# Agent attention with a SoLU layer: every second pair of token tiles takes another way from the activations to the output

## The chip, the cores and the metric

The kernel runs on one NeuronCore of a Trainium2 chip. Five engines work side by side and wait for each other through semaphores: TensorE (PE in the profile, its weight loads PEld) multiplies matrices into PSUM; VectorE (DVE) and ScalarE (ACT) read PSUM and SBUF; GpSimd (POOL) works on SBUF only; SyncE (SP) issues the transfers, which 16 DMA engines carry out. Each engine works through its instructions in the order in which they were written. The metric is the device time of one execution in microseconds (us), as the median of several runs; lower is better.

## The reference

Four batches of 12608 tokens of 128 numbers go through an attention with 49 agents per batch, and the 50432 resulting rows through a feed-forward layer with 1024 hidden columns. All is fp32.

```python
def _attn_ref(q, k, v, agents):
    def sm(a, b):
        s = scale * (a @ b.transpose(0, 2, 1))
        s = s - s.max(-1, keepdims=True)
        e = np.exp(s)
        return e / (e.sum(-1, keepdims=True) + 1e-09)
    agent_v = sm(agents, k) @ v
    return sm(q, agents) @ agent_v

def _moe_ref(x, w_in, w_out, g_ln):
    h = x @ w_in
    e = np.exp(h - np.max(h, axis=-1, keepdims=True))
    solu = h * e / (np.sum(e, axis=-1, keepdims=True) + 1e-09)
    mu, var = mean and variance of solu over its 1024 columns
    return ((solu - mu) / np.sqrt(var + 1e-06) * g_ln) @ w_out
```

## The kernel before

**Phase A**, once per batch: the agents against k and v, in 13 chunks of up to 1024 tokens. Its result is multiplied into `w_in`, so that the first layer becomes one product of 49 attention weights with a matrix of 1024 columns (`bmats`, kept as a high and a low part, `mh` and `ml`). **Phase B**, per 8 tiles of 128 tokens: the attention weights p of each token, turned by TensorE (`pack` to a PSUM bank `px`), split by ScalarE (`b6`, L698) and VectorE (`b7`, L703) into a high and a low part `pn`, and laid into `pT` by four transfers (`b8`, L716).

**Phase C**, per tile of 128 tokens (396 of them), is where the time goes: `c_h` multiplies `pT` with `mh` and `ml` into a PSUM pair `ph` (L757); `c_max` takes the row maximum on VectorE (L761); `c_exp` the exponentials on ScalarE (L771); `c_u` the product u of both on VectorE (L776); `c_sq` the squares on ScalarE (L782). There are two `ph`, so at most two tiles are between their first product and their u. Then u must be turned, so that the 1024 hidden columns lie along the partitions: `c_t` does it with 8 TensorE transposes per tile (L789), into `px` banks, of which there are four. From there u goes to SBUF in a high part `uH` and a low part `uL`. For most halves ScalarE copies (`c_ev`, L808), and GpSimd splits (`c_sph` L817, `c_spl` L821); for the halves named in `DIR` ScalarE writes `uH` itself (L804) and VectorE subtracts (`c_ldir`, L813). `c_w` then multiplies a pair of tiles (256 tokens) with the output weights: 24 products, high by high, low by high and high by low for each of the 8 slices of 128 columns (L837), with the weights stationary. The output comes out with its 128 columns along the partitions. Four tiles are a group: `c_rstd` makes the scale of each token on GpSimd, `sent` brings it through DRAM to all partitions (`dr`, `rB`, L878 and L879), `c_fin` multiplies it in while it empties the bank (L902), `c_out` stores (L918).

**The order of everything** is written out in advance. A planner (`Plan`) takes every operation with its engine, its cost, what it depends on and a due time, counted in tiles, and lays the operations one after the other on each engine; the order of PE, ACT, DVE and POOL is then fixed as it was laid. The due times are constants in the kernel (`BD0` to `DWL`), one for each kind of operation. SP issues its transfers in order too, each held back until what it waits for has happened.

## Time and profile before

The median of three runs is 1538.96 us (1538.89 to 1542.58).

| What | Value |
|---|---|
| span of the profiled execution, first to last instruction | 1535.9 us |
| median of the runs less that span | 3.1 us |
| busy: PE, ACT, DVE, POOL | 1509.6, 1424.4, 1366.4, 1251.6 us |
| mean granted TensorE clock | 0.998 |
| DMA queue q1, share of 16 engines | 33.0% |
| bytes moved | 159.65 MB |

The profiled execution's own time is known by its span alone; 3.1 us is what lies around it if it was a run like the median. A busy PE is a modelled figure: products are pipelined, and the end of each is computed. How fast they follow each other is read from their starts, in the timeline. In the groups the columns are line, engine, operation, output and inputs with their sizes, count, then busy time in us and the mean of one in ns, and idle time of that engine ahead of them.

### The profile page before, as it was taken

The page shows a single profiled execution, that of the slowest core. Times are in us where ns is not written, and L with a number is a line of the kernel's source. Part 1 is how long each engine was busy: PE and PEld are TensorE (multiplying, and loading weights), DVE is VectorE, ACT ScalarE, POOL GpSimd, SP SyncE. Part 2 cuts the span into 40 slices and gives each one's busy share as a digit, 9 for nine tenths or more (in the row PEclk, how much of TensorE's full clock was granted, in tenths as well). Part 3 has the DMA queues.
Part 4 walks back from the last instruction along what each step waited for, and adds up shares of the span by engine and source line. Part 5 has one row for each costly group of instructions (what it writes and reads, how often), then busy time and mean ns, then how long its engine had stood idle before and what let it go on. Part 6 is the DMA issues. An engine that isn't in the chain of part 4 may idle for free.

```text
span 1535.9 us, 35549 instructions
## 1 busy us (share of the span) xinstructions
PE 1509.6 (98%) x12643; PEld 1352.4 (88%) x12643; DVE 1366.4 (89%) x2201; ACT 1424.4 (93%) x2747; POOL 1251.6 (81%) x1613
## 2 busy tenths in 40 slices
...
GB/s 371 190 128 73 146 91 111 96 101 94 95 77 151 111 111 90 139 82 104 82 97 136 106 118 87 128 99 104 68 89 61 87 66 90 72 86 56 63 56 46
DMA packets 114720, 159.65 MB, mean 104 GB/s; under 512 B 16240, under 2 KB 71152, under 8 KB 114544
## 3 DMA queue, kind: packets, MB, share of 16 engines
q1 hardware_dynamic: 114544, 157.39, 33.0%
q8 instruction: 100, 1.64, 0.4%
q14 instruction: 76, 0.62, 0.1%
...
## 4 chain that ended last, share of the span: by engine, by line
PE 73%; ACT 9%; POOL 7%; DVE 5%; issue 4%; DMA 2%; DVEq 0%; SPq 0%; ACTq 0%; POOLq 0%
PE px L837 28%; PE ph L757 18%; PE px L789 17%; ACT e L771 4%; POOL uL L821 3%; PE px L476 2%; PE px L427 2%; PE px L657 2%; ACT sq L782 2%; POOL uH L817 2%; ACT uT L808 2%; DVE u L776 1%; PE px L460 1%; PE px L692 1%; POOL y L856 1%
## 5 line engine op out<-in xcount | busy, mean ns | idle before, releaser
L821 POOL TENSOR_TENSOR uL<-uT,uH 128x1024 fp32r<-128x1024 f32 (+1 forms) x344 | 661.9, 1924 | 25.3
L761 DVE TENSOR_REDUCE nm<-ph 128x1 f32<-128x1024 f32 x396 | 479.2, 1215 | 73.9 <-PE ph L757 72.5
L776 DVE SCALAR_TENSOR_TENSOR u<-ph,e 128x1024 f32<-128x1024 f32 x396 | 480.4, 1218 | 41.9 <-ACT e L771 31.1
L782 ACT ACTIVATE sq<-u,su 128x1024 bf16<-128x1024 f32 x396 | 463.7, 1171 | 23.0 <-DVE u L776 19.7
L771 ACT ACTIVATE e<-ph,nm 128x1024 f32<-128x1024 f32 x396 | 449.0, 1137 | 16.9 <-DVE nm L761 15.3
L837 PE MATMUL px<-uL,wH 128*128 128x256 f32 x1584 | 461.6, 291 | 1.3 <-POOL uL L821 1.3
L837 PE MATMUL px<-uH,wH 128*128 128x256 f32 x1584 | 451.9, 285 | 4.2 <-DVE uL L813 2.0
L837 PE MATMUL px<-uH,wL 128*128 128x256 f32 x1584 | 448.8, 283 | 0.0
L789 PE MATMUL px<-ident,u 128*128 128x128 f32 x3168 | 430.1, 273 | 2.8 <-DVE u L776 1.6
L789 PEld LDWEIGHTS px<-ident,u 128*128 128x128 f32 x3168 | 365.2, 141 | 40.1 <-DVE ob L902 2.5
L757 PE MATMUL ph<-mh,pT 128*128 128x512 f32 x792 | 334.3, 422 | 5.2 <-DMA pT<-pn 2.4
L817 POOL TENSOR_SCALAR uH<-uT 128x1024 fp32r<-128x1024 f32 (+1 forms) x344 | 298.5, 868 | 46.8 <-ACT uT L808 44.7
L837 PEld LDWEIGHTS px<-uH,wH 128*128 128x128 f32 x1584 | 298.8, 189 | 19.4 <-issue 5.7
L808 ACT COPY uT<-px 128x512 f32<-128x512 f32 x541 | 301.6, 592 | 13.0 <-PE px L789 4.8
L757 PE MATMUL ph<-ml,pT 128*128 128x512 f32 x792 | 313.0, 395 | 0.1
L837 PEld LDWEIGHTS px<-uL,wH 128*128 128x128 f32 x1584 | 298.9, 189 | 7.9 <-issue 3.0
L837 PEld LDWEIGHTS px<-uH,wL 128*128 128x128 f32 x1584 | 299.0, 189 | 5.5 <-issue 1.4
L813 DVE TENSOR_TENSOR uL<-px,uH 128x512 fp32r<-128x512 f32 x251 | 167.9, 683 | 9.9 <-ACT uH L804 9.2
L757 PEld LDWEIGHTS ph<-mh,pT 128*128 128x128 f32 x792 | 149.6, 189 | 30.6 <-issue 6.8
L757 PEld LDWEIGHTS ph<-ml,pT 128*128 128x128 f32 x792 | 150.2, 190 | 16.5 <-DVE ml L552 0.6
L804 ACT CAST uH<-px 128x512 fp32r<-128x512 f32 x251 | 147.2, 606 | 2.4 <-PE px L789 2.0
L856 POOL TENSOR_TENSOR y<-x,nhalf 128x4 f32<-128x4 f32 x99 | 100.1, 1011 | 7.7
...
## 6 DMA issues: line engine op xcount, KB each, us to landing
...
```

The source lines that it names most:

```text
L757: nc.tensor.matmul(ph[:, sl], lhs, bmats[b]["mh" if m == 0 else "ml"][:, sl], start=(m == 0), stop=(m == 1))
L761: nc.vector.tensor_reduce(out=nms[x], in_=phs[x], op=ALU.max, axis=AX.X, negate=True)
L771: nc.scalar.activation(out=es[x], in_=phs[x], func=AF.Exp, bias=nms.pop(x), accum_out=st[G]["S"][:, j : j + 1])
L776: nc.vector.scalar_tensor_tensor(out=u, in0=phs[x], scalar=INV, in1=es[x], op0=ALU.mult, op1=ALU.mult, accum_out=su)
L782: nc.scalar.activation(out=sq, in_=u, func=AF.Square, bias=su, scale=-float(DF), accum_out=st[G]["Q"][:, j : j + 1])
L789: nc.tensor.transpose(pt[:, kf * P : (kf + 1) * P], us[x][0][:, k0 * P : (k0 + 1) * P], ident)
L804: nc.scalar.copy(out=uH, in_=pt)
L808: nc.scalar.copy(out=rr[x][:, hf * 4 : hf * 4 + 4, :], in_=pt)
L813: nc.vector.tensor_tensor(out=uL, in0=pt, in1=uH.bitcast(F32), op=ALU.subtract)
L817: nc.gpsimd.tensor_scalar(out=uH, in0=rr[x][:, k0:k1, :], scalar1=1.0, scalar2=0.0, op0=ALU.mult, op1=ALU.add)
L821: nc.gpsimd.tensor_tensor(out=uL, in0=rr[x][:, k0:k1, :], in1=uH.bitcast(F32), op=ALU.subtract)
L837: nc.tensor.matmul(po, wt[:, kf, :], ut[:, kf, :], start=(q == 0), stop=(q == WM - 1))
```

## The change

Pairs of tiles are now of two kinds, taken in turn (`PAT`): Z pairs keep the way described above, Y pairs take a new one. By the instructions of the changed kernel 204 tiles are Z and 192 are Y. Two pairs of one kind make a group of four tiles, so a group spans three pairs of the order, and groups of the two kinds overlap.

For a Y tile, `c_tb` has VectorE turn u in blocks of 32 by 32 in one instruction of 128x1024 elements (SBUF to SBUF, L866). When four Y tiles are turned, `c_mv` issues 16 transfers from SBUF to SBUF, each of 32 partitions by 4 KB, 2.1 MB together, which bring the blocks to the right partitions (`uY`, L873). `c_wy` then multiplies in native fp32: a slice of turned u of 128 hidden columns by 128 tokens is stationary, the fp32 weights `w2` move; 32 products per group in chunks of two (L879). The output has tokens along the partitions; its scale per token is fetched by `c_yp` (one store, four loads of single numbers, L885 and L887), multiplied in by `c_fy` on ScalarE (L894, 31 groups, four instructions each) or VectorE (L896, 17 groups), and stored to a second output by `c_oy` (four stores per group, L905). The rows of the two outputs are put together after the run.

Z tiles lose the direct halves except within the last ten tiles: GpSimd splits all of them. In phase B, `b6` copies to fp32 (L743) and GpSimd makes both parts of p (`b7h` L749, `b7l` L754). Buffers change: k and v have one chunk instead of two, `uH`/`uL` two instead of four, `uT` three instead of four, `pT` four instead of eight. Every due time has a new value; the diff shows one of them.

```diff
+PAT = "ZYZY"
...
+def pair_kinds(n):
+
+    kinds = ["Z" if i < HEADZ or i >= n - 4 else PAT[i % len(PAT)] for i in range(n)]
+    if kinds.count("Y") % 2:
+        kinds[max(i for i in range(n) if kinds[i] == "Y")] = "Z"
+    units, open_ = [], {}
+    for i, k in enumerate(kinds):
+        if k in open_:
+            units[open_.pop(k)][1].append(i)
+        else:
+            open_[k] = len(units)
+            units.append((k, [i]))
+    return units
...
-    UTB = 4
...
+    UTB = 3
+    ZB = 2
+    SB = 6
+    DIR = {(1, 0), (1, 1), (3, 1), (5, 0), (5, 1), (7, 1)}
+    DT0 = 10.8
...
-    DH = -3.24
...
+    DH = -9.08
...
-    PTB = 8
...
+    PTB = 4
...
+    B7G = True
...
-    kpool = ctx.enter_context(tc.tile_pool(name="kpool", bufs=2))
+    kpool = ctx.enter_context(tc.tile_pool(name="kpool", bufs=1))
...
-    gpool = ctx.enter_context(tc.tile_pool(name="gpool", bufs=4))
+    gpool = ctx.enter_context(tc.tile_pool(name="gpool", bufs=ZB))
+    ypool = ctx.enter_context(tc.tile_pool(name="ypool", bufs=2))
...
+    w2 = const.tile([P, NF, C], F32, name="w2")
...
-                old = M1.get(c - 2) if not head else M1.get(c - 7 - c % 2)
+                old = M1.get(c - 1) if not head else M1.get(c - 5 - c % 4)
...
-            nc.scalar.copy(out=r["n", q][:, 0, :w], in_=r["pt", q][:, :w])
+            if B7G:
+                r["f", q] = bpool.tile([P, GT // 2 * P], F32, tag="pf", bufs=2, name=f"pf{b}_{t0}_{q}")
+                nc.scalar.copy(out=r["f", q][:, :w], in_=r.pop(("pt", q))[:, :w])
+            else:
+                nc.scalar.copy(out=r["n", q][:, 0, :w], in_=r["pt", q][:, :w])
+
+        def b7h(q):
+            w = (min(GT, nt - q * GT) + 1) // 2 * P
+            nc.gpsimd.tensor_scalar(out=r["n", q][:, 0, :w], in0=r["f", q][:, :w], scalar1=1.0, scalar2=0.0, op0=ALU.mult, op1=ALU.add)
+
+        def b7l(q):
+            w = (min(GT, nt - q * GT) + 1) // 2 * P
+            pn = r["n", q]
+            nc.gpsimd.tensor_tensor(out=pn[:, 1, :w], in0=r.pop(("f", q))[:, :w], in1=pn[:, 0, :w].bitcast(F32), op=ALU.subtract)
...
+            if B7G:
+                d7 = op("G", lambda q=q: b7h(q), 0.38, dues[5] + 2.5 * q + B7, [a6])
+                d7 = op("G", lambda q=q: b7l(q), 0.7, dues[5] + 2.5 * q + B7 + 0.01, [d7])
...
+    def c_tb(x):
+        G, j = slot[x]
+        if G not in yb:
+            yb[G] = [ypool.tile([P, GT, NF, GT, SQB], F32, tag="tb", name=f"tb{G}"), None]
+        to = yb[G][0][:, :, :, j, :].rearrange("p r k c -> p k r c")
+        nc.vector.transpose(to, us[x][0].rearrange("p (k r c) -> p k r c", r=GT, c=SQB))
+
+    def c_mv(G):
+        tb = yb[G][0]
+        to = yb[G][1] = ypool.tile([P, GT, NF, GT, SQB], F32, tag="uY", name=f"uY{G}")
+        for a in range(GT):
+            for r in range(GT):
+                nc.sync.dma_start(out=to[SQB * r : SQB * (r + 1), a], in_=tb[SQB * a : SQB * (a + 1), r])
+
+    def c_wy(G, a, k0, px=None):
+        if px is not None:
+            st[G]["po"] = px
+        for kf in range(k0, k0 + YC):
+            nc.tensor.matmul(st[G]["po"][:, a * P : (a + 1) * P], yb[G][1][:, a, kf].rearrange("p x c -> p (x c)"),
+                             w2[:, kf, :], start=(kf == 0), stop=(kf == NF - 1))
+
+    def c_yp(G):
+        dr = dpool.tile([P, GT], F32, tag="dy", name=f"dy{G}")
+        yp = st[G]["yp"] = tiny.tile([P, GT], F32, tag="yp", name=f"yp{G}")
+        nc.sync.dma_start(out=dr, in_=st[G]["y"])
+        for x in range(GT):
+            nc.sync.dma_start(out=yp[SQB * x : SQB * (x + 1), :], in_=dr.rearrange("(a c) x -> x c a", c=SQB)[x])
+
+    def c_fy(G, e):
+        ob = obs[G] = opool.tile([P, GT, P], F32, tag="oy", name=f"oy{G}")
+        po, y = st[G]["po"], st[G]["yp"]
+        if e == "A":
+            for j in range(GT):
+                nc.scalar.mul(out=ob[:, j, :], in_=po[:, j * P : (j + 1) * P], mul=y[:, j : j + 1])
+        else:
+            nc.vector.tensor_tensor(out=ob, in0=po.rearrange("p (j d) -> p j d", d=P),
+                                    in1=y.unsqueeze(2).to_broadcast([P, GT, P]), op=ALU.mult)
+
+    def c_oy(G):
+        for z, i in enumerate(units[G][1]):
+            for q in range(2):
+                b, t = divmod(2 * i + q, TB)
+                x, lo = 2 * z + q, (0 if t < TB - 1 else TB * P - N)
+                c0 = b * N + min(t * P, N - P)
+                nc.sync.dma_start(out=out_t[c0 + lo : c0 + P, :].rearrange("(a c) d -> c a d", c=SQB),
+                                  in_=obs[G][SQB * x : SQB * (x + 1), lo // SQB :, :])
+
     def direct(x, hf):
-        return (x % (2 * GT), hf) in DIR or x >= n - TD
+        return (x % (2 * GT), hf) in DIR and x >= n - DT0 or x >= n - TD
...
+        if isY:
+            TBT[x] = op("D", F(c_tb, x), 1.15, at(x, DTB, DTBR, DTBL), [U[x], MV.get(back(G, 2))])
+            if j == GT - 1:
+                a = [TBT[2 * z + q] for z in units[G][1] for q in range(2)]
+                MV[G] = op("S", F(c_mv, G), (5.5, 2.1, 0), x + DMV, a + [WY.get(back(G, 2))])
+                prev = None
+                for q in range(GT * NF // YC):
+                    a, k0 = divmod(q * YC, NF)
+                    f = (lambda px, G=G: c_wy(G, 0, 0, px)) if q == 0 else F(c_wy, G, a, k0)
+                    prev = op("P", f, 0.219 * YC, x + DWY + DWS * q / (GT * NF // YC), [MV[G], prev, FY.get(back(G, 2)) if q == 0 else None] + wready, take=q == 0)
+                    if q == 0:
+                        lead_y = prev
+                WY[G] = prev
...
+            buf = [W.get((zpairs[zix[i] - ZB], 1)) if zix[i] >= ZB else None]
...
+            if isY:
+                YP[G] = op("S", F(c_yp, G), (1.9, 0, 5.0), x + DR, [o, FY.get(back(G, 2))])
+                FY[G] = op("AD", F(c_fy, G), (1.45, 0.62), x + DFY, [WY[G], YP[G], OY.get(back(G, 2))], free=lead_y)
+                OY[G] = op("S", F(c_oy, G), (1.5, 0, 2.5), x + DFY, [FY[G]])
...
-    nc = _bacc.Bacc("TRN2", target_bir_lowering=False, num_devices=1)
+    nc = _bacc.Bacc("TRN2", target_bir_lowering=False, num_devices=1, dynamic_dma_scratch_size=1024)```

Three places show how the order moves. First TensorE, where a tile's first product, its transposes and the output products of an earlier pair meet. Before, in batch 0 (`ph` is the first product's bank pair, `px` the other banks):

```order
L757 MATMUL ph_122<-mh_745,pT_80_0_5029 128x512
L757 MATMUL ph_122<-ml_746,pT_80_0_5029 128x512
L789 MATMUL px_127<-ident,u_5051 128x128 x4
L789 MATMUL px_125<-ident,u_5051 128x128 x4
L837 MATMUL px_124<-uL_4829,wH 128x256
L837 MATMUL px_124<-uH_4828,wL 128x256
L837 MATMUL px_124<-uH_4828,wH 128x256
```

In the changed kernel, in batch 1:

```order
L827 MATMUL ph_126<-mh_4892,pT_24_1_6574 128x512
L827 MATMUL ph_126<-ml_4893,pT_24_1_6574 128x512
L859 MATMUL px_128<-ident,u_6998 128x128 x4
L859 MATMUL px_131<-ident,u_6998 128x128 x4
L879 MATMUL px_129<-w_106,uY_6748 128x128 x4
L955 MATMUL px_130<-uH_6813,wH 128x256
L955 MATMUL px_130<-uL_6814,wH 128x256
L955 MATMUL px_130<-uH_6813,wL 128x256
```

Products of a Y group (L879) stand between those of a Z pair, each into a bank of its own. Second VectorE, two tiles before:

```order
L761 TENSOR_REDUCE nm_8424<-ph_122 128x1
L761 TENSOR_REDUCE nm_8454<-ph_123 128x1
L776 SCALAR_TENSOR_TENSOR u_8476,su_8477<-ph_122,e_8458 128x1024
L813 TENSOR_TENSOR uL_8441<-px_127,uH_8440 128x4x128
L466 COPY eT_6_8502<-px_126 128x512
L776 SCALAR_TENSOR_TENSOR u_8509,su_8510<-ph_123,e_8491 128x1024
L761 TENSOR_REDUCE nm_8518<-ph_122 128x1
```

and in the changed kernel:

```order
L831 TENSOR_REDUCE nm_7361<-ph_127 128x1
L831 TENSOR_REDUCE nm_7376<-ph_126 128x1
L1023 TENSOR_TENSOR ob_7387<-px_130,rB_7111 128x512
L846 SCALAR_TENSOR_TENSOR u_7404,su_7405<-ph_127,e_7381 128x1024
L846 SCALAR_TENSOR_TENSOR u_7415,su_7416<-ph_126,e_7397 128x1024
L528 SCALAR_TENSOR_TENSOR av_5812<-av_5812,fc_5_6870,px_128 128x128
L866 STREAM_TRANSPOSE tb_7267<-u_7415 128x8x4x32
L831 TENSOR_REDUCE nm_7438<-ph_127 128x1
```

The subtraction of a half (L813) is gone, and one block transpose stands behind every two u and ahead of the next two maxima. Third SP's queue, with what each transfer waits for (DMAHW0 to DMAHW7 are the eight semaphores that the transfers use in turn), before:

```order
L918 DMA out_dram<-ob_5441 128x512 [waits DVE_49]
L878 DMA dr_5460<-yr_5448 4x32 [waits DVE_49]
L878 DMA dr_5460<-yr_5448 4x32 [waits DMAHW5_49]
L878 DMA dr_5460<-yr_5448 4x32 [waits DMAHW6_49]
L878 DMA dr_5460<-yr_5448 4x32 [waits DMAHW7_49]
L416 DMA vt_1_6338<-in_v_dram 128x1024 [waits DMAHW0_49,PE_49]
```

and in the changed kernel:

```order
L772 DMA pT_64_0_3488<-pn_64_0_3439 64x2x128
L448 DMA kt_11_3495<-in_kT_dram 128x1024 [waits PE_49]
L873 DMA uY_3498<-tb_3227 32x1024 [waits DVE_49]
L873 DMA uY_3498<-tb_3227 32x1024 [waits DMAHW1_49]
L873 DMA uY_3498<-tb_3227 32x1024 [waits DMAHW2_49]
L873 DMA uY_3498<-tb_3227 32x1024 [waits DMAHW3_49]
L873 DMA uY_3498<-tb_3227 32x1024 [waits DMAHW4_49]
L873 DMA uY_3498<-tb_3227 32x1024 [waits DMAHW5_49]
L873 DMA uY_3498<-tb_3227 32x1024 [waits DMAHW6_49]
L873 DMA uY_3498<-tb_3227 32x1024 [waits DMAHW7_49]
L873 DMA uY_3498<-tb_3227 32x1024 [waits DMAHW0_49]
L873 DMA uY_3498<-tb_3227 32x1024 [waits DMAHW1_49]
```

Ten of these rows are the start of one group's 16; the last two shown reuse the semaphores of the first ones, so each waits until the transfer eight places ahead of it has landed. In all SP issues 2122 transfers in the changed kernel and 1163 before.

More of the change, by code (lines that the diff above doesn't have):

```diff
@@ L129, in run, with token_tiles @@
                     self.push(z)
+TILES_P = 128
+PAT = "ZYZY"
[11 more added lines that the diff above has]
+    return units
+HEADZ = 0
+def token_tiles(b, n):
+    return [(t, min(t * TILES_P, n - TILES_P), 0 if (t + 1) * TILES_P <= n else (t + 1) * TILES_P - n)
+            for t in range((n + TILES_P - 1) // TILES_P)]
 @with_exitstack
@@ L143 @@
     out: bass.AP,
+    out_t: bass.AP,
 ):
@@ L165 @@
     WC = 4
[L167 to L186 removed]
+    BD0 = 5.03
+    BD1 = 15.85
+    BD2 = 7.13
+    BD3 = -20.87
+    BD4 = -1.82
+    BD5 = 2.99
+    DH = -9.08
+    DMX = 6.59
+    DEX = 3.59
+    DU_ = -7.86
+    DSQ = 15.3
+    DT = -0.92
+    DEV = 13.75
+    DLD = 15.0
+    DSP = 16.84
+    DW = 13.2
+    DR = 15.79
+    DF_ = 38.5
+    OUTD = 30.9
+    OUTC = -69.6
     VA = 3
     VA1 = 12
[L189 to L218 removed]
+    QA = 22.03
+    WA = -6.5
+    VLAG = 0.74
+    PTB = 4
+    SHY = 0.31
+    DHR = 5.82
+    DHL = -8.78
+    DMXR = 19.87
+    DMXL = -4.95
+    DEXR = -2.43
+    DEXL = -9.36
+    DUR = -30.26
+    DUL = -10.56
+    DSQR = -50.18
+    DSQL = 4.99
+    DTR = -20.36
+    DTL = -14.16
+    DEVR = -17.55
+    DEVL = 7.51
+    DLDR = -20.48
+    DLDL = -18.62
+    DSPR = -1.34
+    DSPL = -11.65
+    DWR = -2.28
+    DWL = -11.0
+    RBL = 3.14
+    ASP = 0.86
+    MZ = 4.24
+    B7G = True
+    B7 = -4.63
+    DTB = -0.32
+    DMV = -0.88
+    DWY = 11.65
+    DWS = 4.05
+    YC = 2
+    DFY = 5.38
+    DTBR = -5.14
+    DTBL = -8.13
+    ASTART = -4.09
+    AEND = -4.76
     engs = (mybir.EngineType.PE, mybir.EngineType.Activation, mybir.EngineType.DVE, mybir.EngineType.Pool)
@@ L579, in phase_a @@
             kop(c)
-            if not head:
-                kop(c + 1)
             z = c * 2.55
@@ L584, in phase_a @@
                        [K[c], M1.get(c - 1), TT.get(c - 2)], take=True, kind=2)
+            if not head:
+                kop(c + 1)
             E1[c] = op("D", st(p1_max, c), 0.6, at(z + 0.3), [M1[c], bg])
@@ L746, in phase_b @@
             qload(k + 2, dues[0], [prev])
-    us, phs, nms, es, rr, pr, st = {}, {}, {}, {}, {}, {}, {}
+    us, phs, nms, es, rr, pr, st, yb = {}, {}, {}, {}, {}, {}, {}, {}
+    units = pair_kinds(n // 2)
+    slot, kind, unit = {}, {}, {}
+    order = {"Y": 0, "Z": 0}
+    for k, (kd, ps_) in enumerate(units):
+        for z, i in enumerate(ps_):
+            unit[i] = k
+            for j in range(2):
+                slot[2 * i + j] = (k, 2 * z + j)
+                kind[2 * i + j] = kd
     def c_h(x, hf):
@@ L844, in r0 @@
             for z in "txyz":
-                r[z] = tiny.tile([P, GT], F32, tag=z, name=f"{z}{G}")
-            r["yc"] = ycol[G % 2]
+                r[z] = tiny.tile([P, GT], F32, tag=z, bufs=SB, name=f"{z}{G}")
+            if units[G][0] == "Y":
+                r["yc"] = st[G]["y"] = tiny.tile([P, GT], F32, tag="yy", bufs=SB, name=f"yy{G}")
+            else:
+                r["yc"] = ycol[nth[G] % 2]
             gp.tensor_scalar(out=r["t"], in0=st[G]["S"], scalar1=1e-9, scalar2=math.sqrt(1e-6 * DF), op0=ALU.add, op1=ALU.mult)
@@ L955, with back @@
     H, MX, EX, U, SQ, T, EV, LD, SH, SP, W, FIN, RB, TN = ({} for _ in range(14))
-    utl, pol = [], []
+    TBT, MV, WY, FY, OY, OZ, YP, R2 = ({} for _ in range(8))
+    utl, pol = [], {}
+    nth, seen = {}, {"Y": [], "Z": []}
+    for G, (kd, _) in enumerate(units):
+        nth[G] = len(seen[kd])
+        seen[kd].append(G)
+    zpairs = [i for i in range(n // 2) if units[unit[i]][0] == "Z"]
+    zix = {i: z for z, i in enumerate(zpairs)}
+    def back(G, k):
+        z = nth[G] - k
+        return seen[units[G][0]][z] if z >= 0 else None
     ku = 0
@@ L1036 @@
     plan.run(idle)
-    assert all(not z for z in plan.cand.values()) and FIN[n // GT - 1].end is not None
+    assert all(not z for z in plan.cand.values()) and FIN[len(units) - 1].end is not None
     prev = {}
```

198 lines of the change are left out of this document (81 added, 117 removed).

## The prediction

> **What bounds the kernel now.** I read the page's busy times first, then windows, the chain of waits and the waits.
>
> ```profile
> span 1535.9 us, 35549 instructions
> PE 1509.6 (98%) x12643; PEld 1352.4 (88%) x12643; DVE 1366.4 (89%) x2201; ACT 1424.4 (93%) x2747; POOL 1251.6 (81%) x1613
> ```
>
> ```profile
> 0.00:58.00 58.00, 52.74 (x492) 33.66 (x493) 40.91 (x98) 26.44 (x67) 21.02 (x34) 1.00 0.92 327
> 58.00:1526.00 1468.00, 1451.90 (x12118) 1314.65 (x12116) 1324.01 (x2101) 1397.35 (x2680) 1229.96 (x1576) 1.00 0.31 96
> 1200.00:1460.00 260.00, 259.00 (x2144) 236.79 (x2144) 237.35 (x365) 254.78 (x480) 234.34 (x304) 1.00 0.26 73
> 1526.00:1536.00 10.00, 4.96 (x39) 4.12 (x37) 1.45 (x3) 0.58 (x1) 0.60 (x3) 0.90 0.08 23
> ```
>
> ```profile
> PE 73%; ACT 9%; POOL 7%; DVE 5%; issue 4%; DMA 2%; DVEq 0%; SPq 0%; ACTq 0%; POOLq 0%
> ```
>
> ```profile
> DVE nm L761 <- PE ph L757: 72.5, 117, 2.4
> DVE u L776 <- ACT e L771: 31.1, 88, 1.3
> PE ph L757 <- DMA pT<-pn: 2.4, 2, 1.5
> SPq L879 <- DMA dr<-yr: 60.4, 62, 3.3
> ```
>
> The windows' columns are length, then busy PE, PEld, DVE, ACT, POOL, then granted clock, DMA share, GB/s. The 396 tiles run from 58 to 1526: 1468 us, 3.71 per tile. PE is busy 1451.9 of them, and busy here is work: products follow at the pace of their rows (below). The chain is PE for 73%, and VectorE waits for PE (72.5 us for a tile's first product). So TensorE is the bound, with 16 us idle. The third window says what two loaded engines can do in this scheme: PE 259.0 and ScalarE 254.8 of 260.
>
> **The change part by part.** TensorE first. Its paces come from starts in the timeline.
>
> ```profile
> L789 PE MATMUL px<-ident,u 128*128 128x128 f32 x3168 | 430.1, 273 | 2.8 <-DVE u L776 1.6 <-DVE ob L902 0.6 <-ACT uT L808 0.5
> 808.41 0.81 PE L789 MATMUL px<-ident,u 128*128 128x128 f32 x6
> 805.72 0.28 PE L837 MATMUL px<-uL,wH 128*128 128x256 f32 x1
> 806.66 0.28 PE L837 MATMUL px<-uH,wH 128*128 128x256 f32 x1
> 54.33 0.39 PE L532 MATMUL px<-ff,av 128*128 128x128 f32 x2
> 54.55 0.38 PE L928 MATMUL ph<-ones 128*128 128x256 bf16 x2
> ```
>
> Six transposes in 0.81 with the last one's 0.273 give (0.81 - 0.273)/5 = 0.107; nine output products start between 805.72 and 806.66, eight steps of 0.1175. The new product exists once before: phase A's L532, 128x128 by 128 in native fp32, is two records, and what follows starts 0.22 after it. By the order, transposes go from 3168 to 1632 (-1536 x 0.107 = -164.4), split products from 4752 to 2448 (-2304 x 0.1175 = -270.7), and 1536 native ones come (x 0.22 = +337.9). Sum -97.2: TensorE alone gives a span of 1535.9 - 97.2 = 1438.7. Bounds for the native product: two records at the transposes' pace, 0.214 (-9 us on the sum), and 0.39, the whole of L532 with nothing hidden (+261). I take 0.22, since L532 is the same form.
>
> A page speaks against this. The Trainium skill, "FP8 and Floating Point Precision", TensorE Precision Notes, counts four passes for true fp32, and "TensorE: Matmul & The Clock Gate", LDWEIGHTS, gives columns/1.2 ns for a weight load, 107 ns for 128. If every pass loaded its own weights that would be, by an estimate from these pages, 0.43 per product, and the sum +222 instead of -97. L532's two records at 0.22 contradict it; the rival "loads not hidden" below carries what is left of the doubt.
>
> VectorE:
>
> ```profile
> L776 DVE SCALAR_TENSOR_TENSOR u<-ph,e 128x1024 f32<-128x1024 f32 x396 | 480.4, 1218 | 41.9 <-ACT e L771 31.1 <-PE px L789 4.8 <-ACT sq L782 1.0
> L761 DVE TENSOR_REDUCE nm<-ph 128x1 f32<-128x1024 f32 x396 | 479.2, 1215 | 73.9 <-PE ph L757 72.5
> L813 DVE TENSOR_TENSOR uL<-px,uH 128x512 fp32r<-128x512 f32 x251 | 167.9, 683 | 9.9 <-ACT uH L804 9.2
> L703 DVE TENSOR_TENSOR pn<-px,pn 128x256 fp32r<-128x256 f32 x100 | 41.8, 418 | 5.7 <-ACT pn L698 5.5
> L902 DVE TENSOR_TENSOR ob<-px,rB 128x512 f32<-128x512 f32 x98 | 67.0, 683 | 3.3 <-DMA rB<-dr 2.6 <-PE px L789 0.4
> L872 DVE STREAM_TRANSPOSE yr<-ycol 128x32 f32<-128x32 f32 x98 | 19.9, 203 | 0.4 <-POOL ycol L868 0.2
> L525 DVE TENSOR_SCALAR rs<-px 128x1 f32<-128x1 f32 x4 | 0.6, 150 | 0.0
> ```
>
> Gone: 241 of 251 half subtractions (167.9/251 = 0.669 each, -161.2), the p subtraction (-41.8), 48 of 98 closing products (x 0.683 = -32.8) and 48 small transposes (x 0.203 = -9.7). New: 17 closing products of Y groups (+11.6) and 192 block transposes of 128x1024. If these run an element per step like the two rows of 1024 above, 1.22 each: +234.2. Sum +0.3, so VectorE's body stays 1324. From above: L872 takes 203 ns for one block column of 32 and the smallest operation 150; if each of 32 block columns cost the difference, 0.15 + 32 x 0.053 = 1.85, +121 us. From below: a copy at twice the pace, 0.15 + (1.22 - 0.15)/2 = 0.68, -104. I take 1.22, the rows of that size. The waits for the exponentials (31.1) stay, because u still stands right behind the maxima. VectorE's floor is 1324 + 31 + 68 (the head and the tail around the body) = 1423. Its 72.5 us of waiting for first products is where the block transposes now lie.
>
> ScalarE and GpSimd lose work:
>
> ```profile
> L808 ACT COPY uT<-px 128x512 f32<-128x512 f32 x541 | 301.6, 592 | 13.0 <-PE px L789 4.8 <-POOL uH L817 2.5 <-issue 2.1
> L804 ACT CAST uH<-px 128x512 fp32r<-128x512 f32 x251 | 147.2, 606 | 2.4 <-PE px L789 2.0
> L821 POOL TENSOR_TENSOR uL<-uT,uH 128x1024 fp32r<-128x1024 f32 x197 | 472.4, 2398 | 14.5
> L821 POOL TENSOR_TENSOR uL<-uT,uH 128x512 fp32r<-128x512 f32 x147 | 189.6, 1290 | 10.8
> L817 POOL TENSOR_SCALAR uH<-uT 128x1024 fp32r<-128x1024 f32 x197 | 207.1, 1051 | 42.8 <-ACT uT L808 40.8 <-issue 1.9
> L817 POOL TENSOR_SCALAR uH<-uT 128x512 fp32r<-128x512 f32 x147 | 91.4, 622 | 4.0 <-ACT uT L808 3.9
> ```
>
> ScalarE: 143 copies fewer (x 0.557 = -79.7) and 241 casts fewer (x 0.586 = -141.3); 124 products of 128x128, at most a 128x512 copy's 0.557 and at least a quarter of it, I take 0.35: +43. 1424.4 becomes 1246. GpSimd: all 147 half splits go (-281.0), one full split more (+3.4), and 100 splits of p at 128x256: between half of the 128x512 rows (0.96 together) and all of them (1.91), I take 1.15, since a halved row here keeps a fixed part (1.290 against 2.398): +115. 1251.6 becomes 1089. Both are off the bound; the cover is their own slack, 200 and 350 us. What hides the longer way of p (a GpSimd split queued behind a u split of 3.45 us, then SP, then the first product) is the lead of `pT`, now four groups of four tiles instead of eight; PE waited 2.4 us for pT before.
>
> SP and the transfers:
>
> ```profile
> 700.72 2.59 SPq L716 DMA_DIRECT2D pT<-pn  x4
> 707.94 1.35 SPq L878 DMA_DIRECT2D dr<-yr  x4
> 712.64 0.47 SPq L879 DMA_DIRECT2D rB<-dr  x1
> 741.54 0.36 SPq L416 DMA_DIRECT2D vt<-in_v_dram  x1
> 235.07 3.50 DMA pT<-pn
> 608.50 6.64 DMA pT<-pn
> DMA packets 610, 0.34 MB, mean 86 GB/s; under 512 B 72, under 2 KB 576, under 8 KB 609
> q1 hardware_dynamic: 609, 0.33, 32.4%
> DMA packets 1359, 4.97 MB, mean 414 GB/s; under 512 B 149, under 2 KB 149, under 8 KB 1358
> ```
>
> Eight tiles now issue 8 pT transfers (2 x 2.59), 4 dr and 1 rB (1.82), 16 uY, and 13.5 others (dy, 4 yp, 4 stores of Y, 2 of Z, 2.5 loads). At 0.36 each for uY (5.8) and 0.36 to 0.65 for the others (4.9 to 8.8) that is 17.7 to 21.6, and 1.9 for two round trips through DRAM (60.4/62 each): 20 to 24 us of the 27.9 that eight tiles last at a span of 1449. Behind each uY row stand pT, rB and yp of later tiles. The data: 2.1 MB at the rate of the head's 4 KB rows (414 GB/s between 8 and 20 us) 5.1 us, at the rate of pT's SBUF transfers (86 GB/s at a 32.4% share, so 265) 7.9. About as long as the issue; it hides behind the tiles between the last block transpose and the products, some 11 of them.
>
> Head and tail I leave at 58 and 10 us: the last pairs stay Z.
>
> **The sum.** TensorE wants 1438.7, VectorE 1423 if no wait for a first product is left and 1423 + 36 = 1459 if half remain. With two engines this close I take the middle of the two bounds, 1449 (then PE is busy 1354.7 of a body of 1381, 98.1%, and VectorE 95.9%; the third window above had 99.6 and 98.0 side by side). The runs' median lies 3.1 above the span: 1452, with 1425 to 1478 as this case's own range.
>
> **The rivals.**
>
> *VectorE becomes the bound.* For it: three long operations per Y tile in one queue, each with a wait in the ring product, maximum, exponential, u. Against: none of the rows asks for more than 1.22. At 1.5 us per block transpose its floor is 1423 + 54 and, with half the waits, 1513; at 1.85 it is 1543 without any, no faster than now. I give 1495, range 1478 to 1545. The Trainium skill ("VectorE: DVE Perf Modes", The three transpose paths) has 311 ns for a 128x128 bf16 block turn; eight of these would be 2.49 us per tile, an estimate that ends far above the old time, but L872's 203 ns for a quarter of those columns leaves (311 - 203)/96 = 1.1 ns per further column, which agrees with 1.22 rather than with 2.49.
>
> *The uY block makes pT late (slower).* SP works in order: a uY row that waits for VectorE's fourth block transpose, or for a semaphore, holds the pT rows behind it, and 2.1 MB of uY lie ahead of pT in the DMA rings. The two pT landings above took 6.64 us and 3.50, a spread of 3.14. If the lead of `pT` is used up and each of the 48 uY blocks costs the first products that much, the span is 1449 + 48 x 3.14 = 1600, the median 1603. It decides from 1.8 us per block (1539 - 1452 = 87, over 48). For: half the lead of before, a longer way of p through GpSimd, twice the transfers. Against: four groups of `pT` are 16 tiles, some 55 us, and SP keeps 4 to 8 us of every eight tiles free.
>
> *Weight loads of the native products are not hidden (slower).* At 0.39 per product the sum is +164, 1703; it passes the old time from 0.283.
>
> *Nothing waits.* Idle time on PE as before and VectorE at the pace of back-to-back operations: below 1425.
>
> **Chances.** Forecast 0.60; VectorE bound 0.20; late pT 0.12; weight loads 0.04; below 1425 0.04. A measurement of this kernel tells 0.3% from no change: 1534 to 1544. Of the second case 0.02 lies there, of the third 0.01: faster 0.60 + 0.04 + 0.18 = 0.82, same 0.03, slower 0.15. The range 1415 to 1525 holds the forecast, three quarters of the second case and most of the last: 0.78, near enough 8 in 10.
>
> **What would show it.** Right: native products in runs at 0.21 to 0.23; block transposes at 1.2 to 1.3; PE busy at 96% or more of the body and the chain still mostly PE; DVE's waits for first products below 50 us; uY landed within 9 us of its first issue; ScalarE below 1260 and GpSimd below 1110. Wrong: a chain that runs through DVE (second case), PE or DVE waiting for DMA uY, yp or pT (third), PEld filling the gaps between native products (fourth).

## The result: slower by 11%, and the profile after

| | before | changed |
|---|---|---|
| median of four runs each, on one chip | 1539.17 us (1538.89 to 1542.58) | 1708.29 us (1705.46 to 1713.78) |
| ratio, with its 95% interval | | 1.1096 (1.1072 to 1.1119) |
| span of the profiled execution | 1535.9 us | 1711.7 us |
| mean granted TensorE clock | 0.998 | 0.935 |

The forecast was 1452, with a range of 1415 to 1525. Now and then an execution comes out far longer than the others of its kernel and is left out below; one of these, of 3636 us, is of the kernel with an eighth of the data, which leaves that kernel one.

The page of the changed kernel, its span and busy times, its row of granted clocks in 40 slices, and its chain of work:

```profile
span 1711.7 us, 34410 instructions
PE 1482.9 (87%) x11858; PEld 1313.2 (77%) x11858; DVE 1371.7 (80%) x1972; ACT 1283.6 (75%) x2488; POOL 1097.1 (64%) x1525
PEclk9989999989989999998999999899999998889889
PE 39%; DVE 15%; ACT 13%; SPq 11%; DMA 11%; issue 6%; POOL 5%; DVEq 0%; ACTq 0%; POOLq 0%
```

VectorE's busy time is that of before (1371.7 us against 1366.4), ScalarE's and GpSimd's are less; at 80% and below none of them is a bound. PE has fallen from 98% to 87%, and the chain, 73% PE before, now passes through every engine, SP (11%) and the DMAs (11%). That is a kernel that waits for something. The waits name it (us in total, times, longest):

```profile
ACT sq L852 <- DVE u L846: 213.3, 82, 11.9
POOL uH L934 <- ACT uT L925: 210.5, 75, 12.4
DVE ob L1023 <- DMA rB<-dr: 196.6, 25, 12.5
PE px L955 <- DVE ob L1023: 67.3, 9, 9.1
PE px L859 <- DVE ob L1023: 41.9, 7, 11.8
```

The first two rows are the longest, but each of them waits for an engine that is itself waiting. The third is nearer the source: the closing product `ob` of a Z group waits for `rB`, the scales of its four tiles, 25 times and 196.6 us in all; before, that row was one wait of 2.6. `ob` stands in VectorE's queue ahead of the maxima and `u` of the next tiles. While it waits, ScalarE gets no `u`, GpSimd no `uT`, and TensorE no bank (the last two rows).

Why `rB` is late stands in SP's and VectorE's timeline of one such period (start, length, what; in brackets what the engine waited for):

```profile
1467.38 2.71 SPq L772 DMA_DIRECT2D pT<-pn  x4
1470.20 11.61 SPq L873 DMA_DIRECT2D uY<-tb  x16
1481.91 1.99 SPq L905 DMA_DIRECT2D out_dram<-oy  x4
1484.01 2.71 SPq L772 DMA_DIRECT2D pT<-pn  x4
1486.82 1.45 SPq L999 DMA_DIRECT2D dr<-yr  x4
1489.37 0.32 SPq L1000 DMA_DIRECT2D rB<-dr  x1
```

```profile
1474.00 0.21 DVE L993 STREAM_TRANSPOSE yr<-ycol 128x32 f32<-128x32 f32 x1
1483.33 1.23 DVE L831 TENSOR_REDUCE nm<-ph 128x1 f32<-128x1024 f32 x1 [0.15 <-PE ph L827]
1493.11 0.69 DVE L1023 TENSOR_TENSOR ob<-px,rB 128x512 f32<-128x512 f32 x1 [8.55 <-DMA rB<-dr]
```

`yr`, the source of `dr`, is ready at 1474.2. SP is then 4 us into a block of 16 uY transfers that holds it for 11.61; the Y stores and a pT group follow, and `dr` is issued at 1486.8, 12.6 us after it could have been. `rB` lands at 1493.1, 6.3 us after that issue; issued at 1474.2 it would, by the same 6.3 us, have landed at 1480.5 (an estimate), ahead of the 1484.6 at which VectorE begins to wait. By the forecast such a block held SP for 5.8; of the 44 blocks that nothing interrupts, the shortest takes 10.1, the median 10.8 and the longest 16.1.

### The profile page after: what moved, and what is told of

Read it like the earlier page. It is cut to its first block, busy times and chain, and to the rows that moved or that the text cites. A ratio compares the mean times of both kernels' runs of the same rounds, so it can differ in the third digit from the quotient of the medians.

```text
span 1711.7 us, 34410 instructions
## 1 busy us (share of the span) xinstructions
PE 1482.9 (87%) x11858; PEld 1313.2 (77%) x11858; DVE 1371.7 (80%) x1972; ACT 1283.6 (75%) x2488; POOL 1097.1 (64%) x1525
## 4 chain that ended last, share of the span: by engine, by line
PE 39%; DVE 15%; ACT 13%; SPq 11%; DMA 11%; issue 6%; POOL 5%; DVEq 0%; ACTq 0%; POOLq 0%
PE ph L827 10%; PE px L879 8%; PE px L955 7%; ACT e L841 5%; DMA rB<-dr 5%; PE px L859 5%; DVE u L846 5%; SPq L873 5%; DVE nm L831 4%; ACT sq L852 3%; DVE tb L866 3%; SPq L772 3%; ACT uT L925 3%; PE px L470 2%; PE px L519 2%
## 5 line engine op out<-in xcount | busy, mean ns | idle before, releaser
L852 ACT ACTIVATE sq<-u,su 128x1024 bf16<-128x1024 f32 x396 | 459.6, 1161 | 218.0 <-DVE u L846 213.3
L831 DVE TENSOR_REDUCE nm<-ph 128x1 f32<-128x1024 f32 x396 | 471.2, 1208 | 49.4 <-PE ph L827 47.5
L846 DVE SCALAR_TENSOR_TENSOR u<-ph,e 128x1024 f32<-128x1024 f32 x396 | 474.7, 1216 | 32.2 <-ACT e L841 25.6
L841 ACT ACTIVATE e<-ph,nm 128x1024 f32<-128x1024 f32 x396 | 442.8, 1122 | 70.6 <-DVE nm L831 68.3
L938 POOL TENSOR_TENSOR uL<-uT,uH 128x1024 fp32r<-128x1024 f32 x200 | 474.7, 2374 | 14.4
L879 PE MATMUL px<-w,uY 128*128 128x128 f32 x3072 | 401.6, 278 | 5.8 <-DMA uY<-tb 3.6
L879 PEld LDWEIGHTS px<-w,uY 128*128 128x128 f32 x3072 | 379.0, 194 | 18.4 <-issue 6.3
L827 PE MATMUL ph<-mh,pT 128*128 128x512 f32 x792 | 351.3, 444 | 29.2 <-DVE u L846 29.0
L934 POOL TENSOR_SCALAR uH<-uT 128x1024 fp32r<-128x1024 f32 x200 | 209.8, 1049 | 210.6 <-ACT uT L925 210.5
L827 PE MATMUL ph<-ml,pT 128*128 128x512 f32 x792 | 322.9, 408 | 0.0
L955 PE MATMUL px<-uH,wH 128*128 128x256 f32 x816 | 242.4, 297 | 67.3 <-DVE ob L1023 67.3
L859 PE MATMUL px<-ident,u 128*128 128x128 f32 x1632 | 235.1, 283 | 43.7 <-DVE ob L1023 41.9
L925 ACT COPY uT<-px 128x512 f32<-128x512 f32 x398 | 225.1, 590 | 58.0 <-PE px L859 54.4
L859 PEld LDWEIGHTS px<-ident,u 128*128 128x128 f32 x1632 | 202.3, 147 | 72.9 <-DVE ob L1023 44.7
L866 DVE STREAM_TRANSPOSE tb<-u 128x1024 f32<-128x1024 f32 x192 | 237.1, 1238 | 1.0
L955 PE MATMUL px<-uL,wH 128*128 128x256 f32 x816 | 237.8, 291 | 0.0
L955 PE MATMUL px<-uH,wL 128*128 128x256 f32 x816 | 235.0, 288 | 0.0
L955 PEld LDWEIGHTS px<-uH,wH 128*128 128x128 f32 x816 | 158.7, 194 | 74.6 <-issue 72.0
L827 PEld LDWEIGHTS ph<-mh,pT 128*128 128x128 f32 x792 | 157.9, 199 | 64.9 <-DVE u L846 38.8
L1023 DVE TENSOR_TENSOR ob<-px,rB 128x512 f32<-128x512 f32 (+1 forms) x52 | 35.0, 675 | 204.7 <-DMA rB<-dr 196.6
L827 PEld LDWEIGHTS ph<-ml,pT 128*128 128x128 f32 x792 | 157.8, 199 | 20.9 <-issue 0.5
L955 PEld LDWEIGHTS px<-uL,wH 128*128 128x128 f32 x816 | 159.4, 195 | 2.4 <-issue 0.8
```

What stands on the lines that cost most here:

```text
L827: nc.tensor.matmul(ph[:, sl], lhs, bmats[b]["mh" if m == 0 else "ml"][:, sl], start=(m == 0), stop=(m == 1))
L831: nc.vector.tensor_reduce(out=nms[x], in_=phs[x], op=ALU.max, axis=AX.X, negate=True)
L841: nc.scalar.activation(out=es[x], in_=phs[x], func=AF.Exp, bias=nms.pop(x), accum_out=st[G]["S"][:, j : j + 1])
L846: nc.vector.scalar_tensor_tensor(out=u, in0=phs[x], scalar=INV, in1=es[x], op0=ALU.mult, op1=ALU.mult, accum_out=su)
L852: nc.scalar.activation(out=sq, in_=u, func=AF.Square, bias=su, scale=-float(DF), accum_out=st[G]["Q"][:, j : j + 1])
L859: nc.tensor.transpose(pt[:, kf * P : (kf + 1) * P], us[x][0][:, k0 * P : (k0 + 1) * P], ident)
```

## The experiments

The expectations weigh these theories: S, SP's issue time of the uY transfers holds `dr`, `rB` and `pT`; D, the data of a block fills the rings; C, the native fp32 products lower the granted clock.

### Four transfers in place of sixteen

```diff
-            for r in range(GT):
-                nc.sync.dma_start(out=to[SQB * r : SQB * (r + 1), a], in_=tb[SQB * a : SQB * (a + 1), r])
+            nc.sync.dma_start(out=to[:, a], in_=tb[:, a])
```

> The 16 transfers of a uY block become 4 of 128 partitions with the same 2.1 MB (the blocks land on the wrong partitions, so the outputs of the Y tiles are not the reference's; everything else is the change). Theory S (SP's issue time): in the changed kernel a uY transfer takes SP 0.59 us or more, a block 10.3 to 11.6 us, and dr, rB and pT stand behind it; VectorE then waits for rB 196.6 us in total. With 4 issues the block holds SP 2.6 us at most: rB waits below 30 us, the time 1440 to 1480. Theory D (the data of a block fills the DMA rings): nothing changes, 1680 to 1710. Theory C (the native fp32 products lower the granted clock, 0.935 in the changed kernel): the clock stays below 0.95 and the time above 1550.

Measured: 1538.34 us, ratio 0.998 (0.9967 to 0.9993), clock 0.979. The busy row, the wait for `rB`, and from the view of one line the durations (min/median/max, ns) of a uY issue:

```profile
PE 1447.1 (94%) x11858; PEld 1284.9 (84%) x11858; DVE 1368.4 (89%) x1972; ACT 1281.3 (83%) x2488; POOL 1094.8 (71%) x1525
DVE ob L1022 <- DMA rB<-dr: 72.8, 21, 6.1
L872 SPq DMA_DIRECT2D uY<-tb x192: 484/613/2377, 89.8 to 1484.5; - x192
```

At the median a transfer of four times the bytes takes hardly longer to issue: 613 ns. Some take longer, so an uninterrupted block now holds SP 3.3 us at the median, not the 2.6 expected at most. Twelve issues less per block are worth 170 us. That carries S, but only two thirds of the way: the wait for `rB` is still 72.8, and the time 58 us above the 1480 expected.

### An eighth of the data

```diff
-                nc.sync.dma_start(out=to[SQB * r : SQB * (r + 1), a], in_=tb[SQB * a : SQB * (a + 1), r])
+                nc.sync.dma_start(out=to[SQB * r : SQB * (r + 1), a, 0], in_=tb[SQB * a : SQB * (a + 1), r, 0])
```

The products read that one slice for all eight.

> The 16 transfers stay, each with an eighth of its data (one of eight slices of 128 hidden columns; the native products all read that one slice, as many as before, so the outputs of the Y tiles are not the reference's). Theory S: SP issues as many transfers at 0.5 to 0.6 us each, the time stays within 30 us of the changed kernel's 1708. Theory D: an eighth of 2.1 MB frees the rings, 1440 to 1500. Theory C: clock below 0.95, as in the changed kernel.

Measured, in one run: 1716.34 us.

```profile
DVE ob L1023 <- DMA rB<-dr: 197.3, 26, 11.1
L873 SPq DMA_DIRECT2D uY<-tb x768: 507/589/1962, 91.8 to 1660.3; - x192
```

Both rows are those of the changed kernel (196.6; median 590), though each block moves an eighth of the bytes. Theory D falls for the block as the change moves it. The issue costs 0.59 us for 16 KB as for 128 KB.

### The closing product does not wait for rB

```diff
-                                in1=st[G]["rB"][:, j0:j1], op=ALU.mult)
+                                in1=st[G]["rB"][:, j0:j1] if j1 - j0 < GT else win_sb[...], op=ALU.mult)
```

`dr` and `rB` are still sent; only nothing waits for them, except the last group.

> VectorE's closing product of a Z group multiplies with a constant tile instead of rB (the scale of the Z tiles is left out but in the last group); dr and rB are still issued, nothing waits for them. Theory S with rB as the transfer whose lateness costs: the 196.6 us of VectorE's waits for rB go and the time falls to 1460 to 1540. If pT, uY or yp are as late as rB (SP full, whatever waits for it): the wait moves to TensorE's first or native products and the time stays above 1600. Theory C: above 1600 with a clock below 0.95.

Measured: 1543.24 us, ratio 1.0027 (1.0007 to 1.0047), clock 0.976.

```profile
DVE u L846 <- ACT e L841: 49.0, 64, 5.7
DVE nm L831 <- PE ph L827: 39.6, 45, 4.0
ACT oy L894 <- DMA yp<-dy: 34.3, 14, 5.8
PE px L519 <- DMA vt<-in_v_dram: 15.6, 4, 6.3
```

Without the one big wait, 165 us come back (the time is 3 us above the range expected), and the next things that SP sends late show themselves: `yp`, which ScalarE's closing product of the Y groups needs, and the loads of phase A.

### Both edits at once

> The four-transfer block (wrong partitions, same bytes) and the closing product of the Z groups that reads a constant instead of rB, both at once. Each alone gave 1538 and 1543 us with different waits left: the first still 73 us of VectorE waiting for rB, the second only scattered waits. Theory S (SP's issue time is all of the loss, and the sums for the engines were right): the two losses are one, 1440 to 1475 us, PE 97% or more busy, granted clock 0.99 or above although all 3072 records of the native products are there. Rival C (native fp32 products lower the granted clock): clock stays at 0.975 to 0.985, time 1475 to 1510. Rival R (VectorE's and ScalarE's ring is the second bound, forecast too low for it): about 1520, with VectorE's waits spread over the first products and the exponentials as in the run without rB.

Measured: 1454.88 us (1454.32 to 1456.18), ratio 0.9437 (0.9421 to 0.9453). The page's first rows and its chain, a row of windows (length, then busy PE, PEld, DVE, ACT, POOL, granted clock, DMA share, GB/s), and VectorE's two largest waits:

```profile
span 1452.6 us, 33541 instructions
PE 1420.1 (98%) x11858; PEld 1265.5 (87%) x11858; DVE 1366.7 (94%) x1972; ACT 1277.5 (88%) x2488; POOL 1094.9 (75%) x1525
PE 78%; DVE 8%; ACT 7%; issue 3%; DMA 2%; POOL 1%; SPq 1%; DVEq 0%; ACTq 0%; POOLq 0%
58.00:1442.00 1384.00, 1362.25 (x11339) 1227.71 (x11338) 1321.89 (x1872) 1248.63 (x2418) 1069.94 (x1487) 1.00 0.52 165
DVE u L846 <- ACT e L841: 19.4, 54, 1.1
DVE nm L831 <- PE ph L827: 18.1, 31, 1.8
```

This run keeps every instruction of the compute engines, with their work and their order as changed; it lacks 12 issues per block and one kind of wait. It lands 3 us from the forecast of the changed kernel, and 253 us below that kernel. (The forecast was the middle of two bounds 20 us apart, so the last few us of that agreement are luck.) So 253 us is what late transfers cost, and theory C falls with it: all 3072 records of native products are there, and the clock is 0.995.

The cost has two parts. By the two pages, PE is idle 196 us less here than in the changed kernel (span less busy, 32.5 against 228.8), and busy 63 us less, with the same 11858 records. The second part is the clock, which falls where PE has waited long. In the changed kernel, after the wait shown above:

```profile
1493.94 0.55 PE L955 MATMUL px<-uH,wH 128*128 128x256 f32 x1 [7.54 <-DVE ob L1023]
1494.51 0.41 PE L955 MATMUL px<-uH,wL 128*128 128x256 f32 x1
1495.57 0.41 PE L955 MATMUL px<-uL,wH 128*128 128x256 f32 x1
1490.00:1495.00 5.00, 1.06 (x5) 1.09 (x6) 1.89 (x4) 0.03 (x1) 0.04 (x1) 0.50 0.43 145
```

The granted clock is 0.50, and the output products start 0.212 us apart (five steps between the second row and the third), where the trace of before had 0.1175. By the clock's records, 134 us of PE's busy time in the changed kernel lie at 0.50, and 11 in the run of both edits. At full clock half of each would be saved, an estimate of 62 us between the two runs; 63 were measured.

The Trainium skill ("TensorE: Matmul & The Clock Gate", section "HAM oscillation — how this bites in real kernels") warns of PE gaps above some 3.4 us, after which the array runs at a lower clock. The traces agree: the waits for `rB` reach 12.5 us, PE's behind them 11.8, and PE stands idle for more than 3.4 us 29 times in the changed kernel (clock 0.935) and twice here (0.995). Idle time as such does not do it: the run with every third pair, below, is idle 288 us in all, but only twice for that long, and its clock is 0.974.

### The split of p on VectorE again

```diff
-    B7G = True
+    B7G = False
```

> p split on VectorE again (one part of the change undone; the order is planned anew for it), all else as changed, full computation. Theory S (the uY block in SP's queue is the cause): still slow, 1690 to 1760, with VectorE waiting for rB 150 us or more and VectorE's busy time 42 us up. Rival P (the longer way of p holds SP: SP waited 120 us for GpSimd's pn, and dr and rB stand behind): SP's wait for pn falls below 40 us and the time to 1600 or less.

Measured, in one run: 1696.05 us.

```profile
DVE ob L1023 <- DMA rB<-dr: 151.0, 21, 13.0
SPq L772 <- ACT pn L745: 46.0, 12, 7.1
```

SP's wait for `pn` falls from 119.8 to 46.0, though not below the 40 expected, and the time hardly moves. With 16 transfers per block, the longer way of p is at most a small part of what holds `rB`, whose wait is still 151.0. Whether it explains some of the 72.8 us that are left with four transfers was not tried.

### The planner is told what SP's work takes

The planner of the changed kernel puts 5.5 us on a block, 0.24 on a pT group, 1.5 on the Y stores. The trace shows 10.8 at the median, 2.7 and 2.0. The block is planned as four pieces of four transfers, so that others may pass between, each due two tiles after the last, and each native product waits for its own piece alone; the landings are longer, and all other due times stay.

```diff
-            pT_op[groups[g]] = op("S", lambda q=q: b8(q), (0.24, 0.13 if k else 0, 3.0), ...
+            pT_op[groups[g]] = op("S", lambda q=q: b8(q), (2.6, 0, 5.0), ...
...
-                MV[G] = op("S", F(c_mv, G), (5.5, 2.1, 0), x + DMV, ...
+                for z in range(GT):
+                    mv.append(op("S", F(c_mv, G, z), (2.6, 0, 6.0), x + DMV + 2.0 * z, ...
```

> The change with the planner told what SP was measured to need (uY block 10.4 us instead of 5.5, pT group 2.6 instead of 0.24, Y stores 2.0 instead of 1.5, Z stores 0.9 instead of 0.8, yp 2.3 instead of 1.9) and the uY block planned as four pieces of four transfers, so that dr, rB and pT can go between them; the result is the full computation. Theory S, if it is the order of SP's queue: 1450 to 1530. If SP is simply full (its issues add up to some 25 us of every 27.9): 1550 to 1650. Theory C: above 1600.

Measured: 1619.5 us, ratio 1.0513 (1.0495 to 1.0532).

```profile
DVE ob L1024 <- DMA rB<-dr: 61.0, 15, 5.8
PE px L880 <- DMA uY<-tb: 31.9, 14, 6.0
```

A third of the 253 us comes back by planning alone; the wait for `rB` is down to 61.0, and a new one, of TensorE for uY, stands beside it. The time lies in the range that was expected of an SP that is simply full. That reading does not hold: two of the next runs issue the same 16 transfers per block and are over 100 us faster.

### SP's order, the issue times, and the due times

SP's instructions are the only ones that the kernel does not hold to the planner's order. Three runs separate that order, the planned times and the due times. The first fixes the order and changes nothing else:

```diff
-    engs = (..., mybir.EngineType.DVE, mybir.EngineType.Pool)
+    engs = (..., mybir.EngineType.DVE, mybir.EngineType.Pool, mybir.EngineType.SP)
```

> The changed kernel with one edit: SP's instructions keep the planner's order. Holds, landings and due times stay as in the change (block 5.5 us, pT 0.24, oy 1.5). If the free order of SP alone is the fault: below 1560. If the wrong holds and due times are (the planner thinks SP nearly idle and puts dr and rB behind the blocks by their due times): still 1600 to 1750, VectorE waiting for rB over 100 us.

Measured, in one run: 1734.5 us, with 194.2 us of waiting for `rB` (26 times). A fixed order is worth nothing here, with the old plan behind it. The second has this edit and also the true issue times, landings of 3 to 7.5 us counted from the start of the issue, the block in four pieces as before, `dr` and `rB` (and `dy` and `yp`) as two steps each with a due time of their own, 6.5 tiles behind the group's last tile where it was 15.8, two other constants of the planner (`MARGIN`, `HOLD`), and all the other due times chosen anew, by a search for the planner's shortest plan. So the order of all engines is another:

```diff
-                RB[G] = op("S", sent, (2.4, 0, RBL), x + DR, [TN[G], FIN.get(back(G, 2))])
+                o = op("S", sent[0], (1.45, 0, LDR + 1.0), x + DSR, [TN[G], FIN.get(back(G, 2))])
+                RB[G] = op("S", sent[1], (0.45, 0, LRB), x + DSR, [o])
...
+    LPT, LUY, LDR, LRB, DSR, DMS = 7.0, 7.5, 3.0, 4.0, 6.51, -2.03
```

> Full computation, same pairs on the new way, 16 transfers per block as in the change. SP's instructions now keep the planner's order (until now SP's was left free), and the planner is told the measured issue times (uY 2.7 us per four, pT 2.7, oy 2.0, ob 0.95, dr 1.45, rB 0.45) and landings of 3 to 7 us; the due times are chosen anew for it. Theory S: dr and rB get in front of the blocks, VectorE's wait for rB falls below 40 us and the time to 1450 to 1500. Rival T (SP's total of some 25 us of the 28 that eight tiles last is too much in any order): 1540 to 1620, as in the run with true issue times in the free order (1619.5), and the wait only moves to uY or pT.

Measured: 1500.27 us (1495.11 to 1502.29), ratio 0.9726 (0.9696 to 0.9756), with the full computation and 16 transfers per block. It is faster than both kernels. Its busy row, VectorE's wait for `rB`, and SP around one block:

```profile
PE 1440.8 (96%) x11844; PEld 1269.8 (85%) x11844; DVE 1376.7 (92%) x1983; ACT 1280.1 (86%) x2465; POOL 1096.4 (73%) x1525
DVE ob L1033 <- DMA rB<-dr: 16.1, 10, 3.3
1004.64 1.41 SPq L1006 DMA_DIRECT2D dr<-yr  x4
1008.76 0.34 SPq L1010 DMA_DIRECT2D rB<-dr  x1
1009.20 2.49 SPq L875 DMA_DIRECT2D uY<-tb  x4
1011.74 2.35 SPq L911 DMA_DIRECT2D out_dram<-oy  x4
1014.13 7.50 SPq L875 DMA_DIRECT2D uY<-tb  x12
```

`dr` and `rB` now leave ahead of the block. By the trace SP issues for 1153.8 of the 1496.9 us, so it is not full. The third is this kernel with SP's order left free again:

> The run with the planned order on SP (1500.3) with one edit undone: SP's order is left free again, with the true holds and the new due times kept. If the fixed order carries the gain: 1540 to 1640, with dr or rB behind blocks and VectorE waiting for rB over 50 us. If the holds and due times carry it: within 15 us of 1500.

Measured: 1507.37 us, ratio 0.9786 (0.977 to 0.9802), 13.4 us of waiting for `rB`. So the new plan carries the gain, above all what the run of 1619.5 lacked (due times, landings, the two steps, the two constants), and the fixed order adds some 7 us. Which part of the plan does most was not taken apart.

### What sixteen issues cost under the better plan

The run of 1500 with four transfers per block, as in the first experiment:

> The run with true issue times and new due times (1500.3), with the block moved by four transfers of 128 partitions instead of sixteen of 32 (same bytes, wrong partitions; nothing else changed, rB is used as it should be). If what is left between 1500 and the 1454.9 of the run with both edits is SP's issue time: 1450 to 1470, VectorE's wait for rB below 10 us. If it lies in the new order of the engines (waits in the ring, more work in VectorE's queue): 1485 to 1500.

Measured: 1472.39 us (1470.39 to 1472.6), ratio 0.9557 (0.9541 to 0.9573). It falls between the two expectations. Of the 45 us between 1500 and 1455, 28 are issue time. The remaining 17 are not the wait for `rB`, which is 0.2 us here. The run differs from that of 1455 in the order of all engines, and PE is busy 12 us longer (1432.1 against 1420.1); that the new order costs them is likely, but what in it does was not looked for.

### Two that lost: through DRAM, and every third pair

To save issues without wrong partitions, a block can be written to DRAM by one transfer and read back by four:

```diff
+        nc.sync.dma_start(out=dt, in_=yb[G][0])
...
-            nc.sync.dma_start(out=to[SQB * r : SQB * (r + 1), a], in_=tb[SQB * a : SQB * (a + 1), r])
+        nc.sync.dma_start(out=to[SQB * a : SQB * (a + 1)].rearrange("p s k x t -> p s (k x t)"), in_=dt[a])
```

> Full computation, every second pair on the new way, SP in the planner's order as in the run with the planned order (1500). The block goes through DRAM: one transfer writes tb (128 partitions), four of 32 partitions read it back in the new order, so 5 issues instead of 16; due times chosen anew. Theory S (what is left of the loss, 1500 against 1455, is SP's issue time): SP spends 1.8 to 3.0 us per block instead of 10.4 to 11.6, VectorE's waits for rB and PE's for uY together below 15 us, time 1445 to 1480. Rival D (now 4.2 MB per block go through the rings, 10 to 16 us at 265 to 414 GB/s, and pT, rB and yp wait behind them): waits for DMA on PE and VectorE above 60 us in all, time above 1510.

Measured: 1791.38 us, ratio 1.163 (1.1613 to 1.1648). The queue's row (packets, MB, share of 16 engines), then SP's largest waits:

```profile
q1 hardware_dynamic: 202656, 346.26, 70.5%
SPq L897 <- DMA dy<-yy: 133.3, 29, 11.4
SPq L773 <- DMA uY<-dt: 86.9, 50, 3.4
```

The issues do shrink (0.376 for the write, 0.430 for each read, 2.1 us per block). But 346 MB move in place of 246, and SP stands 133.3 us for the 2 KB of `dy`, up to 11.4 at a time, with `yp`, uY and pT behind it. PE and VectorE themselves wait 12.6 us for uY and 24.8 for `rB`, below the 60 that rival D asked for. The rest of the loss is spread over the ring and was not taken apart, and the due times are this run's own, so how much of it the data cost stays open.

The other is the kernel of 1500 us with every third pair on the new way, and due times chosen anew for it:

```diff
-PAT = "ZYZY"
+PAT = "ZZY"
```

> As the run with the planned order on SP, but every third pair (64 of 198) on the new way instead of every second. PE's sum shrinks to two thirds: -65 us, span 1471. SP has one block of 11 us per 12 tiles instead of per 8: some 30 of 43 us. Theory S: no wait for rB, 1475 to 1505, faster than before. Rival T (the order and not the load is what matters): the same waits as with every second pair, above 1530.

Measured: 1871.92 us, ratio 1.2144 (1.2122 to 1.2166).

```profile
POOL pn L750 <- ACT pf L744: 271.1, 89, 13.5
DVE nm L832 <- PE ph L828: 177.8, 161, 4.8
DVE u L847 <- PE px L860: 166.0, 120, 10.4
```

No wait for `rB` is among the large ones, so it says nothing against S, and nothing for it: this order loses in other places, GpSimd waiting for `pf` with the splits of u behind it, and the ring waiting for both. Why its plan fits the chip so badly stays open.

## Why the prediction was wrong

**The step that failed is the one on SP.** It priced a uY row at 0.36 us, the issue of a load from DRAM (`vt`), and so a block at 5.8, eight tiles at "20 to 24 us of the 27.9". The nearest row was another, already in the trace before: pT is the one transfer there that also goes from SBUF to SBUF. From the views of one line, of before and of the changed kernel:

```profile
L716 SPq DMA_DIRECT2D pT<-pn x400: 590/599/1851, 36.4 to 1504.0; - x134
```

```profile
L873 SPq DMA_DIRECT2D uY<-tb x768: 507/590/2087, 90.7 to 1657.6; - x192
```

The prediction even quoted pT's groups of four at 2.59 us, 0.65 each; sixteen of those are 10.4, and the blocks take 10.8 at the median. With 10.4 in place of 5.8 its own sum is 25 to 29 us of 27.9, hardly any slack. Measured, the total was missed by less: all of SP's issues in the changed kernel add up to 1131.9 us, 22.9 per eight tiles against 17.7 to 21.6 forecast, so SP would still have had some time left. What failed is above all the length of the piece: a block holds whatever stands behind it for 10.8 us and more, not for 5.8. The Trainium skill ("DMA: Bandwidth & Descriptors", section "Anatomy of one DMA", which describes the GpSimd path) has about 50 ns for the sequencer's dispatch; that is no help for SP here, where 590 is measured.

**The second gap was order.** The prediction saw that `rB` stands behind the uY rows, and put its lateness at nothing. The sum asked whether SP has time enough, not what stands behind a block when it comes, nor what stands behind the instruction that then waits: `ob`, 50 small products of 0.685 us, held VectorE's queue for 196.6 us. With the same 16 issues, a plan in which `rB` leaves ahead of the block gives 1500.

**The rivals.** "The uY block makes pT late (slower)" had the mechanism, SP working in order, and the right side of the old time, at a chance of 0.12. Its victim was wrong (`rB`, not `pT`) and its price too low: 3.14 us per block where (1711.7 - 1452.6)/48 = 5.4 were lost. What spoke against it, 4 to 8 us of SP free in every eight tiles, came from the sum with the short block, and free time in a queue does not say when it comes. "VectorE becomes the bound" did not come: 80% busy, and 94% even in the run without late transfers.

**TensorE's sum was right.** Native products were priced at 0.22:

```profile
1581.85 3.12 PE px L879 x28
703.95 3.57 PE px L879 x32
```

These are two pieces of the chain of the changed kernel, 0.1115 per record and 0.223 per product, so "weight loads not hidden" falls, and with it the estimate of 0.43. In the run of both edits PE's body is 1362.25 us busy against 1354.7 forecast, and the span 1452.6 against 1449. In the changed kernel PE shows 1482.9 busy for the same work, since part of it ran at half the clock (above); busy time is no measure of work where the clocks differ.

**VectorE's sum was right**, block transposes included (priced at 1.22):

```profile
L866 DVE STREAM_TRANSPOSE tb<-u 128x1024 f32<-128x1024 f32 x192 | 237.1, 1238 | 1.0
```

Its body in the run of both edits is 1321.9 against 1324. GpSimd has 1097 against 1089. ScalarE has 1283.6 against 1246, above the 1260 that was to show this step right. The groups that the change touches moved as priced (the copies and casts of u from 448.8 to 230.8; Y products 35.4 against 43). What failed is the subtraction: ScalarE's records overlap, and its busy time counts each moment once. The durations of all its groups add up to 1691.4 us before and 1487.9 in the changed kernel, 203.5 less, but busy time falls by only 140.8. It is off the bound, so it cost nothing.

**"uY landed within 9 us of its first issue"** could not hold, since the issue alone takes longer. The data, 5.1 to 7.9 us by the forecast, did not matter: an eighth of it gave the same time.
